# A fused convolution and feed-forward kernel: all tap products ahead of the fifth copies, part buffers in thirds, one more group on seven products

## The chip, the core and the metric

The kernel runs on one core of one Trainium2 chip. The metric is the device time of one execution in microseconds (us). Three runs of the kernel before took 988.49, 989.33 and 987.34 us, a median of 988.49. The profiled execution spans 988.2 us, and all views below are of that execution. The engines are called as the profile calls them: PE is the matrix engine (PEld its weight loads), DVE the vector engine, ACT the scalar engine, POOL the engine that here mostly issues transfers, and SP the engine that issues the plain loads and stores.

## The reference, cut to what matters

The input is x with 8 sequences of 4224 rows of 192 channels. The reference is two steps:

```
w   = softmax(weight, axis=-1)                      # 8 heads, 7 taps
y   = sum over k of w[h, k] * x_pad[s + k, channels of h]   # causal convolution, 24 channels a head
xn  = (y - mean(y)) / sqrt(var(y) + 1e-6) * g_ln
out = y + relu(xn @ w_ch1) @ w_ch2                   # 192 -> 768 -> 192
```

All numbers are float32. The two matrix products make up the arithmetic of the matrix engine. The kernel folds g_ln and the subtraction of the mean into the first weight matrix, and it multiplies by the inverse root of the variance only at the end, because relu commutes with a positive factor.

## The kernel before

**Groups.** The rows are cut into 18 groups, numbered 0 to 17; most of them hold 128 partitions times 16 rows. Groups 0 to 2 are small or odd. Groups from 3 on are "fast": their second matrix product ("down") is computed by seven products of half-size blocks instead of eight (the scheme of Strassen and Winograd). Groups 5 to 16 (`MIXED`, line 81) also compute four of the six hidden chunks of the first matrix product ("up") by seven products; the other two chunks are computed plainly. Group 4 computes its whole "up" plainly.

**What a group does.** In group g the matrix engine works first on "up" (`up`, line 538, or `up_mixed`, line 591) and then on "down" (`down_fast`, line 714). Beside that work the other engines prepare later groups and finish the earlier one:

- The convolution of group g+2 begins in "down" of group g. ACT multiplies the first tap into `y` (`first_tap`, line 376) and the second tap into a buffer `tb` (`second_tap`, line 393). When the last head of the second tap is done, POOL issues two transfers that add `tb` to `y` in halves. Line 756 to 760 say how many of these 16 ACT instructions stand behind each of the six products that are listed there.
- DVE adds the other five taps of group g+1 (`conv`, line 408) in "up" of group g, then transposes `y` into `yt`.
- ACT copies the results of the products from PSUM to SBUF, scales the output rows of group g-1 (`scale`, line 826), and POOL issues transfers that add these rows to the output in memory (`add_to_out`).
- SP stores `y` to the output and loads the next `x` (`store_y`, `load_x`).

**"Up" in mixed groups.** `up_mixed` computes its seven products in a fixed order in two sets of PSUM banks, `chain` and `other`. Three results have to be added to blocks that lie in SBUF already. For each of them ACT copies the product to a part buffer, and POOL issues a transfer that adds the buffer to the block (`close`, line 614): to c11 from a room in the pool of `tb`, to c22 from a room in the pool of `cs`, to c21 from the first room again. A room holds J * D = 3072 elements a partition, and a part uses PAIR = 2 thirds of it. After the plain chunk, DVE turns c21 and the plain chunk into relu(.) minus a block (`lower_sum`, line 702); "down" reads that in its second product.

**"Down" in fast groups.** The six calls of `product` behind line 756 are, in order: c11, c22, a part, one that stays in PSUM, c21 (the fifth) and two more. ACT copies each product's three pieces. Behind the fifth, in a mixed group, POOL issues a transfer that adds a part to c21 (`close_by_dma`, line 748, the rows `cs<-part` of the profile). `finish_fast` (line 796) then transposes the result into `ot`: its half 0 needs the rows that this transfer adds to, its half 1 needs a DVE addition first. At the end of the group DVE computes the sums of `yt` that the next mixed "up" needs (`sums_of_y`, line 575, a generator of which the last step runs inside the next "up").

**Order.** The schedule is written by hand: every engine runs its instructions in the order of the program text, and waits where a tile is not ready. POOL's queue, SP's queue and DVE's program are therefore in the order in which the Python code calls them. The pools `tb`, `cs`, `ot` and `ys` have one buffer each, `y` and `x` two.

Of the kernel before, what the change touches and what calls it, by code (L numbers as in the profile page):

```python
# [16 lines left out]
def kernel(  # L17
# [32 lines left out]
    H, K = weight.shape  # L50
# [12 lines left out]
    NQ = P // C  # L63
# [9 lines left out]
    NG = len(groups)  # L73
# [4 lines left out]
    NFAST = max(fast.values())  # L78
    T = C // 2

    MIXED = range(5, NG - 1)
    PAIR = NF // 2 - 1
    HJ = J // 2
    EARLY = 10
# [26 lines left out]
    bpool = ctx.enter_context(tc.tile_pool(name="tb", bufs=1))  # L111
    cpool = ctx.enter_context(tc.tile_pool(name="cs", bufs=1))
# [64 lines left out]
    room = hpool.tile([P, NF * J * P], F32, tag="ht", name="room")  # L177
# [213 lines left out]
    tb = {}  # L391
# [16 lines left out]
    def conv(g, k0=1, k1=K, heads=(0, H)):  # L408
        n = groups[g][2]
        t = xg[g]  # L410
        for k in range(k0, k1):
            for h in range(*heads):
                cs = slice(h * GRP, h * GRP + GRP)
                nc.vector.scalar_tensor_tensor(  # L414
                    out=y[g][:, 0:n, cs], in0=t[:, k : k + n, cs], scalar=taps[:, h, k : k + 1],
                    in1=y[g][:, 0:n, cs], op0=ALU.mult, op1=ALU.add,
                )
# [173 lines left out]
    def up_mixed(g, last_sum):  # L591


        W = HJ * C
        assert groups[g][2] == fast[g] == 2 * HJ and PAIR * W == 512
        hidden_tile(g)
        a = ht[g][0]
        a11, a12, a21, a22 = quarters_of_y(g)
        b11, b12, b21, b22 = quarters_of_w1()
        s1, s2, s3 = ysums[g]  # L600
        (c11, c12), (c21, c22) = [
            [a[:, h, e, 0:PAIR].rearrange("p f q j t -> p f q (j t)") for e in range(2)]
            for h in range(2)
        ]

        def parts(pool, tag):
            room = pool.tile([P, J * D], F32, tag=tag, name=f"parts_{tag}{g}")
            return room[:, 0 : PAIR * NQ * W].rearrange("p (f q w) -> p f q w", q=NQ, w=W)

        def evict(banks, dst, relu=False):  # L610
            src = banks.rearrange("p q (f w) -> p f q w", w=W)
            nc.scalar.activation(dst, src, AF.Relu) if relu else nc.scalar.copy(dst, src)  # L612

        def close(c, part):
            whole = "p f q w -> p (f q w)"
            add_by_dma(c.rearrange(whole), part.rearrange(whole))

        def plain(f, banks):
            rows_of_tiles(banks, yt[g][:, 0 : 2 * HJ], w1[:, :, f * P : f * P + P])
            evict_up(g, f, slice(0, 2 * HJ), banks)  # L620


        chain, other = take_set(), take_set()
        turn[0] += 4
        done = groups[g - 1][2]
        first, second = parts(bpool, "tb"), parts(cpool, "cs")
        rows_of_tiles(chain, a11, b11, True, False)
        evict(chain, c11)
        rows_of_tiles(other, a12, b21)
        evict(other, first)  # L630
        close(c11, first)
        rows_of_tiles(chain, s2, w1sums[:, 1], False, False)
        evict(chain, c21)
        scale(g - 1, 0, 1)
        conv(g + 1, 2, 3)
        next(last_sum)
        rows_of_tiles(other, s3, w1sums[:, 2], True, False)
        evict(other, c22)
        scale(g - 1, 1, 2)
        rows_of_tiles(chain, s1, w1sums[:, 0], False, False)  # L640
        evict(chain, second)
        close(c22, second)
        scale(g - 1, 2, 3)
        rows_of_tiles(other, a22, w1sums[:, 3], False)
        evict(other, first)
        close(c21, first)
        scale(g - 1, 3, 4)
        rows_of_tiles(chain, s2, b22, False)
        evict(chain, c12, True)
        nc.scalar.activation(c11, c11, AF.Relu)  # L650
        scale(g - 1, 4, 7)
        conv(g + 1, 3, 6)
        plain(PAIR, other)
        nc.scalar.activation(c22, c22, AF.Relu)
        scale(g - 1, 7, 10)
        add_to_out(g - 1, 0, 8)
        lower_sum(g, (PAIR,))
        lower_sum(g, range(PAIR))
        conv(g + 1, 6, K)
        plain(PAIR + FC, chain)  # L660
        scale(g - 1, 10, done)
        add_to_out(g - 1, 8, done)
# [51 lines left out]
    def down_fast(g):  # L714
        n = fast[g]
        t = width(g)
        w = n * T
        a = ht[g][0]
        flat = cpool.tile([P, NC, NFAST * C], F32, tag="cs", name=f"cs{g}")[:, :, 0 : n * C]
        order = "p c (h j t) -> p c h j t" if t == C else "p c (j h t) -> p c h j t"  # L720
        cs = flat.rearrange(order, h=2, t=t)
        part = cpool.tile([P, CH, NFAST * T], F32, tag="part", name=f"part{g}")[:, :, 0:w]
        part = part.rearrange("p c (j t) -> p c j t", t=t)

        parts = [part, a[:, 1, 0].rearrange("p f q j t -> p (f q) j t")[:, 0:CH]]
        banks = [take_bank() for c in range(CH) for i in range(2)]

        def product(bank, left, right, to, first):
            for c in range(CH):
                dst = banks[2 * c + bank]  # L730
                for f in range(FC):
                    for q in range(NQ):
                        nc.tensor.matmul(  # L733
                            dst[C * q : C * q + C, 0:w], right[:, f, C * c : C * c + C],
                            left[:, f, q], start=(first and f == 0), stop=(f == FC - 1),
                            skip_group_check=True,
                        )
                if to is not None:
                    nc.scalar.copy(  # L739
                        to[:, c], dst[:, 0:w].rearrange("p (j t) -> p j t", t=t)  # L740
                    )

        b = quarters_of_w2()
        c11, c21 = cs[:, 0:CH, 0], cs[:, 0:CH, 1]
        c12, c22 = cs[:, CH:NC, 0], cs[:, CH:NC, 1]
        todo = [(tap, h) for tap in (first_tap, second_tap) for h in range(H)] if g + 2 < NG else []

        def close_by_dma(c, part):
            add_by_dma(*(v.rearrange("p c j t -> p c (j t)") for v in (c, part)))

        def some_taps(times):
            for tap, h in todo[:times]:
                tap(g + 2, heads=(h, h + 1))
            del todo[:times]

        taps_behind = [3, 3, 3, 3, 2, 2]
        if g in MIXED:
            taps_behind = [1, 4, 4, 5, 2, 0]
        elif g + 1 in MIXED:
            taps_behind = [4, 4, 4, 4, 0, 0]  # L760
        product(0, a[:, 0, 0], b[0], c11, True)
        some_taps(taps_behind[0])
        product(1, a[:, 1, 0], w2sums[:, 2], c22, True)
        some_taps(taps_behind[1])
        product(1, a[:, 1, 1], w2sums[:, 3], parts[0], False)
        some_taps(taps_behind[2])
        product(1, a[:, 0, 1], b[2], None, True)
        some_taps(taps_behind[3])
        if g in MIXED:
            transpose(g + 1)  # L770
            moments(g + 1, 0, EARLY)
        elif g + 1 in MIXED:
            moments(g + 1)
            if g + 1 == MIXED[0]:
                sums_of_quarters(w1sums, *quarters_of_w1())
        half_sum(g, (1, 1), (1, 1), (1, 0), ALU.add)
        half_sum(g, (0, 0), (1, 1), (0, 0), ALU.add)
        half_sum(g, (0, 1), (0, 1), (1, 1), ALU.subtract)
        for c in range(CH):
            nc.vector.tensor_tensor(  # L780
                c11[:, c], c11[:, c], banks[2 * c + 1][:, 0:w].rearrange("p (j t) -> p j t", t=t),
                op=ALU.add,
            )
        product(0, a[:, 1, 1], w2sums[:, 1], c21, False)
        if g + 1 == NG:
            finish_fast(g, 0, flat, cs, parts)
        if g in MIXED:
            close_by_dma(c21, parts[0])
        some_taps(taps_behind[4])
        product(0, a[:, 0, 0], w2sums[:, 0], parts[1], False)  # L790
        some_taps(taps_behind[5])
        product(0, a[:, 0, 1], b[3], c12, False)
        some_taps(len(todo))
        return flat, cs, parts
# [96 lines left out]
    for g in range(NG):  # L891
        if g + 2 < NG and g not in (3, 4):
            load_x(g + 2)
        mixed, last = g in MIXED, g + 1 == NG
# [41 lines left out]
        parts = down_fast(g)  # L936
# [6 lines left out]
        if mixed:  # L943
            moments(g + 1, EARLY)
        later = sums_of_y(g + 1) if g + 1 in MIXED else iter(())
        if not last:
            finish_fast(g, 0, *parts)
            next(later, None)
        finish_fast(g, 1, *parts)
        if not last and not mixed and g + 1 not in MIXED:  # L950
            moments(g + 1)
        if not last and g % 2 == 0:
# [35 lines left out]
```

## Time and profile before

| | us or share |
|---|---|
| runs (three) | 988.49, 989.33, 987.34 |
| profiled span | 988.2 |
| PE busy | 969.5 (98%) |
| DVE busy | 854.3 (86%) |
| ACT busy | 623.3 (63%) |
| POOL busy | 178.0 (18%) |
| granted clock of the matrix engine | 0.999 |
| one "up", plain (group 4), from its first matrix instruction to that of "down" | 31.1 |
| one "up", seven products (group 5) | 28.6 |
| one mixed group (groups 5 to 16), from "up" to "up" | 56.03 to 57.47 |

The last three rows come from the timeline of PE. In the profile, "out<-in" names the tiles that an instruction writes and reads; `room` is the large tile that holds the hidden blocks, `parts_tb` and `parts_cs` are the part buffers, `ps` is PSUM. A matrix product in float32 appears as two records for each instruction of the program, so that 48 records are 24 instructions. A row of the waits reads "who waited <- who ended the wait: us in total, times, longest".

### The profile page before, as it was taken

The page shows a single profiled execution, that of the slowest core. Times are in us where ns is not written, and L with a number is a line of the kernel's source. Part 1 is how long each engine was busy: PE and PEld are TensorE (multiplying, and loading weights), DVE is VectorE, ACT ScalarE, POOL GpSimd, SP SyncE. Part 2 cuts the span into 40 slices and gives each one's busy share as a digit, 9 for nine tenths or more (in the row PEclk, how much of TensorE's full clock was granted, in tenths as well). Part 3 has the DMA queues.
Part 4 walks back from the last instruction along what each step waited for, and adds up shares of the span by engine and source line. Part 5 has one row for each costly group of instructions (what it writes and reads, how often), then busy time and mean ns, then how long its engine had stood idle before and what let it go on. Part 6 is the DMA issues. An engine that isn't in the chain of part 4 may idle for free.

```text
span 988.2 us, 35674 instructions
## 1 busy us (share of the span) xinstructions
PE 969.5 (98%) x16050; PEld 659.8 (67%) x16050; DVE 854.3 (86%) x1477; ACT 623.3 (63%) x1034; POOL 178.0 (18%) x317
## 2 busy tenths in 40 slices
PE   7999999999999999999999999999999999999997
PEld 6886445556758585766758576676857566685787
DVE  6999886899899898989999898989989898998507
ACT  5625646364867758585875858586685848675451
POOL 2002500115111041112211041111301141110200
PEclk9999999999999999999999999999999999999999
DMA  8233752664797869779677977969696786675141
GB/s 201 95 121 130 116 164 36 209 157 130 139 250 145 239 130 191 194 153 253 143 219 145 208 178 143 260 131 241 143 236 148 147 237 135 160 147 93 18 67 67
DMA packets 26279, 156.07 MB, mean 158 GB/s; under 512 B 3215, under 2 KB 8591, under 8 KB 17294
## 3 DMA queue, kind: packets, MB, share of 16 engines
q0 software_dynamic: 19456, 96.25, 50.3%
q1 hardware_dynamic: 6366, 57.54, 15.2%
q8 instruction: 126, 2.06, 0.8%
q14 instruction: 27, 0.22, 0.1%
q10 hardware_dynamic: 304, 0.00, 0.0%
HBM read 38.95 MB, written 50.33 MB: 90 GB/s over the span
## 4 chain that ended last, share of the span: by engine, by line
issue 44%; PE 32%; DMA 11%; POOL 8%; DVE 4%; ACT 2%; POOLq 0%; SPq 0%; ACTq 0%; DVEq 0%
PE ps L532 16%; PE ps L733 11%; DMA y<-tb 7%; PE ps L680 5%; DVE y L414 3%; DMA xg<-in_x_dram 2%; POOL room L589 2%; POOL out_dram L835 2%; POOL cs L589 1%; ACT parts_tb L612 1%; POOL y L403 1%; DMA room<-parts_tb 1%; POOL d L458 1%; DMA ga<-in_moe_g_ln_dram 0%; DVE room L698 0%
## 5 line engine op out<-in xcount | busy, mean ns | idle before, releaser
L414 DVE SCALAR_TENSOR_TENSOR y<-xg,taps,y 128x384 f32<-128x384 f32 (+4 forms) x734 | 368.1, 579 | 12.1 <-issue 8.9
L532 PE MATMUL ps<-yt,w 32*128 32x512 f32 (+5 forms) x4320 | 334.2, 461 | 2.9 <-ACT parts_tb L612 1.9
L532 PEld LDWEIGHTS ps<-yt,w 32*128 32x128 f32 x4320 | 213.7, 185 | 116.5 <-issue 95.4
L733 PE MATMUL ps<-room,w2sums 128*32 128x256 f32 (+2 forms) x4320 | 233.7, 374 | 0.4 <-issue 0.3
L733 PEld LDWEIGHTS ps<-room,w2sums 128*32 128x32 f32 x4320 | 140.9, 110 | 87.7 <-DVE room L698 2.3
L698 DVE TENSOR_TENSOR room<-room 128x1024 f32<-128x1024 f32 (+2 forms) x144 | 160.4, 1186 | 42.0 <-ACT part L739 23.3
L733 PE MATMUL ps<-room,w 128*32 128x256 f32 (+2 forms) x3240 | 179.3, 374 | 0.0
L733 PEld LDWEIGHTS ps<-room,w 128*32 128x32 f32 x3240 | 104.6, 110 | 72.8 <-ACT ot L828 9.1
L739 ACT COPY cs<-ps 128x256 f32<-128x256 f32 (+2 forms) x180 | 63.3, 366 | 111.8 <-PE ps L733 111.1
L522 ACT ACTIVATE room<-ps 128x2048 f32<-128x2048 f32 (+4 forms) x54 | 79.8, 1477 | 55.2 <-PE ps L532 55.1
L532 PE MATMUL ps<-ysums,w1sums 32*128 32x256 f32 x1728 | 98.4, 377 | 4.0 <-ACT parts_tb L612 4.0
L828 ACT ACTIVATE ot<-ot,r 128x192 f32<-128x192 f32 x248 | 96.2, 448 | 0.0
L532 PEld LDWEIGHTS ps<-ysums,w1sums 32*128 32x128 f32 x1728 | 87.5, 185 | 12.8 <-ACT parts_tb L612 8.3
L612 ACT COPY room<-ps 128x2048 f32<-128x2048 f32 x36 | 67.3, 1868 | 39.6 <-PE ps L532 37.1
L707 DVE SCALAR_TENSOR_TENSOR room<-room 128x1024 f32<-128x1024 f32 x36 | 43.0, 1223 | 45.0 <-ACT room L522 24.5
L387 ACT ACTIVATE y<-xg,taps 128x384 f32<-128x384 f32 (+4 forms) x137 | 71.7, 590 | 11.2 <-DMA out_dram<-y 8.5
L835 POOL DMA_DIRECT2D out_dram<-ot x40 | 34.0, 1077 | 238.2 <-ACT ot L828 187.6
L441 DVE BATCH_NORM_STATS2 st<-y 128x6 f32<-128x192 f32 x264 | 70.8, 342 | 0.0
L612 ACT COPY parts_tb<-ps 128x2048 f32<-128x2048 f32 x24 | 44.8, 1866 | 27.3 <-DMA y<-tb 18.5
L803 DVE STREAM_TRANSPOSE ot<-cs 128x512 f32<-128x512 f32 (+2 forms) x90 | 55.8, 670 | 6.2 <-DMA cs<-part 3.7
L425 DVE STREAM_TRANSPOSE yt<-y 128x3072 f32<-128x3072 f32 (+4 forms) x19 | 56.2, 2957 | 5.1 <-PE ps L532 3.0
L400 ACT ACTIVATE tb<-xg,taps 128x384 f32<-128x384 f32 x112 | 59.5, 605 | 0.0
(104 smaller groups left out, 702.4 us busy)
## 6 DMA issues: line engine op xcount, KB each, us to landing
xg<-in_x_dram SPq DMA_DIRECT2D x12, 2112.0 KB, 14.8
room<-parts_tb POOLq DMA_DIRECT2D x24, 1024.0 KB, 9.3
y<-tb POOLq DMA_DIRECT2D x28, 768.0 KB, 9.1
out_dram<-ot POOLq DMA_DIRECT2D x27, 768.0 KB, 7.8
out_dram<-y SPq DMA_DIRECT2D x12, 1536.0 KB, 9.7
room<-parts_cs POOLq DMA_DIRECT2D x12, 1024.0 KB, 7.5
cs<-part POOLq DMA_DIRECT2D x12, 384.0 KB, 4.5
xg<-in_x_dram POOLq DMA_DIRECT2D x2, 2112.0 KB, 17.8
```

The costliest lines, as they stand in the source:

```text
L387: nc.scalar.mul(dst, src, tap)
L400: nc.scalar.mul(tb[g][:, 0:n, cs], xg[g][:, 1 : 1 + n, cs], taps[:, h, 1:2])
L414: nc.vector.scalar_tensor_tensor(out=y[g][:, 0:n, cs], in0=t[:, k : k + n, cs], scalar=taps[:, h, k : k + 1], in1=y[g][:, 0:n, cs], op0=AL ...
L425: nc.vector.transpose(yt[g][:, 0:n, c0:c1].rearrange("p j c t -> p j (c t)"), y[g][:, 0:n, C * c0 : C * c1])
L441: nc.vector.bn_stats(out=sums[g][:, j, :], in_=y[g][:, j, :])
L522: nc.scalar.activation(dst, src, AF.Relu)
L532: nc.tensor.matmul(banks[:, q, i * w : i * w + w], right[rows, c, P * i : P * i + P], left[rows, :, c, :], start=(first and c == 0 and i = ...
L612: nc.scalar.activation(dst, src, AF.Relu) if relu else nc.scalar.copy(dst, src)
L698: nc.vector.tensor_tensor(a[:, *dst, f], a[:, *left, f], a[:, *right, f], op=op)
L733: nc.tensor.matmul(dst[C * q : C * q + C, 0:w], right[:, f, C * c : C * c + C], left[:, f, q], start=(first and f == 0), stop=(f == FC - 1 ...
L739: nc.scalar.copy(to[:, c], dst[:, 0:w].rearrange("p (j t) -> p j t", t=t))
L828: nc.scalar.mul(ots[g][:, j, :], ots[g][:, j, :], rstd[g][:, j : j + 1])
```

## The change

The change has five edits.

1. `MIXED` begins at group 4, so that group 4 computes "up" with seven products. The sums of the first weight matrix (`w1sums`) are then built in "down" of group 3, and the lists of taps move with it.
2. In mixed groups the fourth product is followed by seven ACT tap products instead of five, and none is left behind the fifth. So all 16 stand ahead of the copies of the fifth product, and the two transfers `y<-tb` stand on POOL's queue ahead of `cs<-part` instead of behind it.
3. The part of c21 is copied in two pieces: each goes into the unused last third of one of the two rooms, and each has a transfer of its own.
4. Half of the last tap (four of the eight heads) is computed by DVE ahead of `lower_sum` instead of behind it.
5. The three sums of `yt` are computed by DVE ahead of half 0 of `finish_fast` instead of behind it.

```
-    MIXED = range(5, NG - 1)
+    MIXED = range(4, NG - 1)
...
-            return room[:, 0 : PAIR * NQ * W].rearrange("p (f q w) -> p f q w", q=NQ, w=W)
+            return room.rearrange("p (f q w) -> p f q w", q=NQ, w=W)
...
-        first, second = parts(bpool, "tb"), parts(cpool, "cs")
+        rooms = parts(bpool, "tb"), parts(cpool, "cs")
+        first, second = (r[:, 0:PAIR] for r in rooms)
...
-        evict(other, first)
-        close(c21, first)
+        for i, room in enumerate(rooms):
+            one, third = slice(i, i + 1), room[:, PAIR : PAIR + 1]
+            evict(other, third, i=one)
+            close(c21[:, one], third)
...
         conv(g + 1, 3, 6)
+        conv(g + 1, 6, K, heads=(0, H // 2))
         plain(PAIR, other)
...
         lower_sum(g, (PAIR,))
         lower_sum(g, range(PAIR))
-        conv(g + 1, 6, K)
+        conv(g + 1, 6, K, heads=(H // 2, H))
...
         if g in MIXED:
-            taps_behind = [1, 4, 4, 5, 2, 0]
+            taps_behind = [1, 4, 4, 7, 0, 0]
...
-        if not last:
-            finish_fast(g, 0, *parts)
-            next(later, None)
-        finish_fast(g, 1, *parts)
+        next(later, None)
+        for half in range(last, 2):
+            finish_fast(g, half, *parts)
```

## The prediction

> **What bounds the kernel.** I read the shares first, then the waits, then the timeline of PE, then that of all engines across one mixed group.
>
> ```profile
> PE 969.5 (98%) x16050; PEld 659.8 (67%) x16050; DVE 854.3 (86%) x1477; ACT 623.3 (63%) x1034; POOL 178.0 (18%) x317
> ```
>
> PE is the bound; only its work and its stalls count. The waits say where it stalls:
>
> ```profile
> PE ps L532 <- ACT parts_tb L612: 5.9, 12, 1.2
> ...
> ACT parts_tb L612 <- DMA y<-tb: 18.5, 11, 2.5
> ...
> ACT parts_tb L612 <- DMA room<-parts_tb: 4.7, 3, 1.6
> ...
> DVE room L707 <- ACT room L522: 24.5, 12, 2.7
> DVE room L707 <- DMA room<-parts_tb: 20.5, 12, 2.3
> ...
> DVE ot L803 <- DMA cs<-part: 3.7, 4, 1.7
> ```
>
> PE waits for ACT's copies into the `tb` room, and ACT waits for the transfers that still read that room: 11 times `y<-tb`, 3 times the part of c11. DVE idles ahead of `lower_sum`. PE's timeline prices a group:
>
> ```profile
> 181.59 31.18 PE L532 MATMUL ps<-yt,w 32*128 32x512 f32 x288
> 212.70 4.09 PE L733 MATMUL ps<-room,w 128*32 128x256 f32 x72
> ...
> 240.31 5.46 PE L532 MATMUL ps<-yt,w 32*128 32x256 f32 x96
> 245.59 7.95 PE L532 MATMUL ps<-ysums,w1sums 32*128 32x256 f32 x144
> 253.36 2.77 PE L532 MATMUL ps<-yt,w1sums 32*128 32x256 f32 x48
> 255.95 2.77 PE L532 MATMUL ps<-ysums,w 32*128 32x256 f32 x48
> 258.54 10.48 PE L532 MATMUL ps<-yt,w 32*128 32x512 f32 x96
> 268.95 4.09 PE L733 MATMUL ps<-room,w 128*32 128x256 f32 x72
> 272.86 7.95 PE L733 MATMUL ps<-room,w2sums 128*32 128x256 f32 x144
> ```
>
> Starts count here. Plain "up": 212.70 - 181.59 = 31.1. Seven products: 268.95 - 240.31 = 28.6. Group 5 has hardly a stall and takes 56.03 (next start 296.34); groups 5 to 16 sum to 922.00 - 240.31 = 681.7, so 12 x 55.95 = 671.4 of work and some 10.3 of stalls. They are: the two ysums sections take 7.77 unstalled, but 7.96 to 9.27 in groups 6 to 16, 7.0 in sum (`y<-tb`); 0.82, 0.83 and 0.79 ahead of the plain chunk in groups 8, 11 and 14, 2.4 in sum (part of c11); the rest is scattered tenths. Last, the end of one group:
>
> ```profile
> 265.85 1.23 DVE L707 SCALAR_TENSOR_TENSOR room<-room 128x1024 f32<-128x1024 f32 x1 [2.44 <-ACT room L522]
> 269.30 2.36 DVE L707 SCALAR_TENSOR_TENSOR room<-room 128x1024 f32<-128x1024 f32 x2 [2.23 <-DMA room<-parts_tb]
> ...
> 289.38 1.30 POOL L589 DMA_DIRECT2D cs<-part  x1 [15.19 <-ACT cs L739]
> 290.39 2.10 POOL L403 DMA_DIRECT2D y<-tb  x2
> ...
> 295.39 1.90 DVE L803 STREAM_TRANSPOSE ot<-cs 128x512 f32<-128x512 f32 x3 [0.66 <-DMA cs<-part]
> ...
> 302.78 1.87 ACT L612 COPY parts_tb<-ps 128x2048 f32<-128x2048 f32 x1 [1.63 <-DMA y<-tb]
> ```
>
> The three adds on POOL's queue land at 295.27, 299.00 and 302.68 by the trace: one behind the other, and ACT waits for the last.
>
> **What the Trainium skill says.** "DMA: Bandwidth & Descriptors", section "Queues, rings and completion order": each of 16 transfer engines consumes a queue's descriptors in order and takes turns between queues by packet. The trace agrees for POOL's queue (the landings above, 3.7 apart). The same page, "Why a DMA increments its semaphore by 16 and not by 1": all engines have to finish. By the packet records 14 of 16 finish the last `y<-tb` by 300.84, but one at 302.35. The same page, "Latency and other measured facts", says that some engines are usually slower; here one lags in most transfers, and the 16 KB packets of the instruction queue may be why.
>
> **The change part by part.**
>
> *Seven products in group 4.* 31.1 - 28.6 = 2.5 saved on PE. The four sums `w1sums` (0.95 each, 3.7 at their spacing) move into group 3's DVE, between its moments and its half sums. There DVE idled 6.9 ahead of the half sums and has moments (4.2) to pull in as well, so 7.9 fills 6.9 and the half sums start about 1 late, at 167.3. PE's fifth product starts at 170.5 and needs three of them (3.2), one at a time: nothing lost, at most 0.5. On POOL the store of `y` and the load of `x` leave some 7 earlier with `y<-tb`; the memset behind the load then waits until about 192, ahead of group 4's first part transfer (189), whose block ACT needs at about 202 and which takes 7.5: 0 to 0.5. I count 2.2.
>
> *Taps.* Two ACT instructions (0.52 each at their spacing) move ahead of the fifth product's copies: the last tap ends at 286.9 instead of 290.1, the first of these copies is 0.9 late, the third, at 288.7, not. PE's sixth product begins at 288.4 with the bank copied first, so nothing is lost. `y<-tb` is issued at 287.1, 3.3 earlier and ahead of `cs<-part`, so it lands 2.5 to 4.5 earlier; ACT waited at most 2.5. The 7.0 go (6 to 7).
>
> *Thirds.* One copy of 2048 (1.87) becomes two of 1024 (about 1.0 each, from the row of a 1024 copy at L522): 0.1 on an ACT that waits 0.3 for PE there: free. POOL issues one transfer more (0.85 of an engine 18% busy). The wait on c11's part goes: 2.4.
>
> *Half a tap ahead of `lower_sum`.* 4 x 0.53 = 2.1 of DVE fills the idle 2.4 and 2.2 there. By itself it costs nothing, and it frees 2.1 later.
>
> *Sums ahead of half 0.* 2.8 of DVE work fills the wait for `cs<-part`.
>
> *What is given back.* `cs<-part` now lands last of the three. It is issued at 289.4 as before, behind 1.5 MB. Let T be its landing after the start of PE's next "up". From it DVE's path runs: 3 transposes, addition, 3 transposes (4.8), 8 taps 4.2, sum 0.9, 24 taps 12.7, and now 4 taps more, 2.1: 24.7, then three `lower_sum` of 1.15 to T + 28.2. PE needs the last of these at 272.86 - 240.31 + 0.43 = 33.0, so PE stalls by T - 4.7. Lower bound of T: the three transfers take 13.3 from first issue to last landing (289.38 to 302.68), so 287.1 + 13.3 = 300.4, T = 4.1: no stall. Upper bound: the slow transfer engine is busy without a gap from the output add to the last `y<-tb`, in group 5 with x's load until 291.3; then the order changes nothing, the last landing stays at 302.7, T = 6.3, and the stall is 1.6. By group, the gap between that load's landing and the first packets of the three adds (issue + 2.2) is 0 in group 5, 1.4, 0.3, 0.5, 1.6, 1.6, 1.1, 0.8, 1.5, 1.2 in 6 to 14; there is no load in 15. Taking it from the last landings (5.9 to 7.2 after the next "up" starts) and summing what is above 4.7 gives 7.3 for all groups. But a stall also moves PE's next start, and so takes itself from the next T: half, 3.6, where the slow engine has no gap. I take 4.2.
>
> **Sum.** 988.2 - 7.0 - 2.4 - 0.5 (scattered) - 2.2 + 4.2 = 980.3 against the profile's span; the span stands 0.3 below the median of the runs, so I forecast 980.
>
> **Rivals.**
> (a) *Nothing is given back*: T stays near 4.1. For it: the data are the same and start 3.3 earlier. Against: the packets of the slow engine. 988.2 - 9.9 - 2.3 = 976.
> (b) *Most is given back*: the slow engine has no gap in any group, stall 0.8 a group in 11 groups: 976 + 9 = 985.
> (c) *Slower*: the add of c21 ends the wait. If T stays at 6.3 whatever PE does, the stall is 1.6 in 11 groups, 17.6, against 12.2 saved: 993.5. It decides from T = 4.7 + 12.2 / 11 = 5.8. For it: the last landing now is 5.9 to 7.2 after the "up". Against: the gaps, and that landings are paced by the previous "up", not by the stalled "down".
> (d) *The thirds or early taps don't move the wait*, and group 4 alone gains: 986. Against: POOL's order of issue shows `y<-tb` first.
>
> **How the numbers follow.** Likeliest, partly given back (977.5 to 983.5): 0.45; (a) 0.25; (b) 0.14; (c) 0.11, with a part of it near no change; (d) 0.05. The range 975.5 to 987 leaves out most of (c) and the tail of (a). A measurement of this kernel tells 0.2% (2 us) from no change: faster 0.84, same 0.07, slower 0.09.
>
> **What would show it.** Right: the waits of ACT for `y<-tb` and for `room<-parts_tb` are gone; group 4's "up" takes 28.6 to 29.2; DVE waits for `cs<-part` at L808 in all mixed groups, 3 to 6 each, and hardly ahead of `lower_sum` (L712); some groups show PE waiting for DVE at its second "down" product, up to 1. Wrong: PE waits there in all groups for over 1, or ACT's scaling of the output waits for DVE in the next "up", or the first ysums section still takes over 8.

## The result and the profile after

The changed kernel took 977.22 us (median of four runs, 976.89 to 978.04), the kernel before 988.91 in the same comparison, 11.7 us more. The ratio is 0.9885, with a 95% interval from 0.9867 to 0.9902: 1.15% faster. The profiled span is 975.6 us.

The page's first line after, engine by engine:

```profile
PE 961.7 (99%) x16194; PEld 665.4 (68%) x16194; DVE 854.3 (88%) x1480; ACT 633.9 (65%) x1052; POOL 188.5 (19%) x334
```

DVE's work is the same to a tenth (854.3 us). The span is 12.6 us shorter: PE's busy time fell by 7.8 and its idle time by 4.8. The busy figure doesn't part work from stalls here, because a row of matrix instructions that is held up for some tenths still counts as busy (before, the rows lost 9.4 us to `parts_tb`, 7.0 and 2.4, of which the list of waits has 5.9). The starts of PE's rows do, and they follow below. All waits of PE over the whole execution (who waited <- who ended it: us in total, times, longest):

```profile
PE ps L364 <- POOL room L292: 4.9, 1, 4.9
PE ps L329 <- DVE room L245: 1.7, 1, 1.7
PE ps L738 <- issue: 1.0, 1, 1.0
PE ps L532 <- DVE yt L425: 0.7, 1, 0.7
PE ps L320 <- DMA xg<-in_x_dram: 0.5, 1, 0.5
```

The wait for ACT's copies into `parts_tb` has left the list, and nothing has come in its place: L364, L329 and L320 are the set-up ahead of group 0, the wait of 0.7 for `yt` stood in the list before with the same figure, and the wait of 1.0 is in the last group. The chain that ended last says it in another way. Here is its first line after:

```profile
PE 95%; DVE 2%; DMA 2%; issue 0%; ACT 0%; SPq 0%
```

Before, that line began with "issue 44%; PE 32%; DMA 11%; POOL 8%": the chain ran back through transfers and through time in which an engine waited for nothing that the profile shows ("issue"). Now it runs almost wholly through PE. PE's timeline in groups 4 and 5:

```profile
180.95 5.46 PE L532 MATMUL ps<-yt,w 32*128 32x256 f32 x96
186.24 7.95 PE L532 MATMUL ps<-ysums,w1sums 32*128 32x256 f32 x144
...
209.59 4.09 PE L738 MATMUL ps<-room,w 128*32 128x256 f32 x72
213.50 7.95 PE L738 MATMUL ps<-room,w2sums 128*32 128x256 f32 x144
...
236.93 5.46 PE L532 MATMUL ps<-yt,w 32*128 32x256 f32 x96
242.21 7.95 PE L532 MATMUL ps<-ysums,w1sums 32*128 32x256 f32 x144
249.98 2.77 PE L532 MATMUL ps<-yt,w1sums 32*128 32x256 f32 x48
252.57 2.77 PE L532 MATMUL ps<-ysums,w 32*128 32x256 f32 x48
255.16 10.48 PE L532 MATMUL ps<-yt,w 32*128 32x512 f32 x96
265.57 4.09 PE L738 MATMUL ps<-room,w 128*32 128x256 f32 x72
```

Group 4's "up" now takes 209.59 - 180.95 = 28.6, as group 5's does (265.57 - 236.93). Every group from 4 to 16 takes 55.97 or 55.98 from start to start; before, groups 5 to 16 took 56.03 to 57.47. So the account is: groups 5 to 16, 681.7 to 671.7, 10.0 less; group 4, 58.7 to 56.0, 2.75 less; 0.65 less ahead of group 4 and 0.8 more behind group 16. The sum is 12.6 less, as the spans say. The 0.65 lies ahead of the first "up" and the 0.8 in the last group; these runs explain neither.

The end of group 5, from the timeline of all engines after:

```profile
283.74 1.74 POOL L403 DMA_DIRECT2D y<-tb  x2 [12.93 <-ACT cs L744]
...
285.93 1.28 POOL L589 DMA_DIRECT2D cs<-part  x1 [0.46 <-ACT cs L744]
...
296.80 1.90 DVE L808 STREAM_TRANSPOSE ot<-cs 128x512 f32<-128x512 f32 x3 [4.28 <-DMA cs<-part]
...
298.47 1.87 ACT L613 COPY parts_tb<-ps 128x2048 f32<-128x2048 f32 x1 [0.77 <-PE ps L532]
```

`y<-tb` leaves 2.2 us ahead of `cs<-part`. ACT's copy at L613 waits for PE now, no longer for a transfer. DVE waits 4.28 for `cs<-part`, where it waited 0.66. DVE's idle time has moved rather than gone: ahead of `lower_sum` it was 45.0 us in all (24.5 and 20.5 in the waits before) and is 3.2 now, while the waits for `cs<-part` have grown from 3.7 to this:

```profile
DVE ot L808 <- DMA cs<-part: 40.6, 10, 4.4
```

These waits cost PE nothing: DVE's chain from the wait to `lower_sum` still ends in time, as its own timeline shows for group 5's "up", behind the end of group 4:

```profile
240.80 1.90 DVE L808 STREAM_TRANSPOSE ot<-cs 128x512 f32<-128x512 f32 x3 [4.06 <-DMA cs<-part]
...
245.46 4.28 DVE L414 SCALAR_TENSOR_TENSOR y<-xg,taps,y 128x384 f32<-128x384 f32 x8
...
250.53 14.91 DVE L414 SCALAR_TENSOR_TENSOR y<-xg,taps,y 128x384 f32<-128x384 f32 x28
265.35 3.49 DVE L712 SCALAR_TENSOR_TENSOR room<-room 128x1024 f32<-128x1024 f32 x3
268.76 2.20 DVE L414 SCALAR_TENSOR_TENSOR y<-xg,taps,y 128x384 f32<-128x384 f32 x4
```

`lower_sum` (L712) has no idle time ahead of it in this group. Its last instruction ends at 268.8. PE wants the last block 0.43 after the start of the second product of "down" (the time of the eight records that need only the block before it), and that product begins 213.50 - 209.59 = 3.91 after the start of "down": at 265.57 + 3.91 + 0.43 = 269.9. That leaves some 1.1 us.

### The profile page after: what moved, and what is told of

Same layout as the page of the kernel before. It is cut to its first block, busy times and chain, and to the rows that moved or that the text cites. A ratio compares the mean times of both kernels' runs of the same rounds, so it can differ in the third digit from the quotient of the medians.

```text
span 975.6 us, 36012 instructions
## 1 busy us (share of the span) xinstructions
PE 961.7 (99%) x16194; PEld 665.4 (68%) x16194; DVE 854.3 (88%) x1480; ACT 633.9 (65%) x1052; POOL 188.5 (19%) x334
## 4 chain that ended last, share of the span: by engine, by line
PE 95%; DVE 2%; DMA 2%; issue 0%; ACT 0%; SPq 0%
PE ps L532 48%; PE ps L738 41%; PE ps L685 5%; DMA xg<-in_x_dram 2%; DVE y L414 2%; PE ps L320 1%; DMA ga<-in_moe_g_ln_dram 0%; DVE yt L425 0%; PE ps L345 0%; DVE y L847 0%; PE ps L350 0%; PE ps L332 0%; DVE y L389 0%; ACT w L355 0%; DVE ot L872 0%
## 5 line engine op out<-in xcount | busy, mean ns | idle before, releaser
L532 PE MATMUL ps<-yt,w 32*128 32x256 f32 (+5 forms) x4224 | 318.7, 453 | 0.7 <-DVE yt L425 0.7
L532 PEld LDWEIGHTS ps<-yt,w 32*128 32x128 f32 x4224 | 209.0, 185 | 102.7 <-issue 84.7
L703 DVE TENSOR_TENSOR room<-room 128x1024 f32<-128x1024 f32 (+2 forms) x141 | 156.9, 1184 | 35.4 <-ACT part L744 24.9
L532 PE MATMUL ps<-ysums,w1sums 32*128 32x256 f32 x1872 | 103.3, 374 | 0.0
L613 ACT COPY room<-ps 128x2048 f32<-128x2048 f32 x39 | 72.8, 1867 | 45.3 <-PE ps L532 43.9
L532 PEld LDWEIGHTS ps<-ysums,w1sums 32*128 32x128 f32 x1872 | 95.9, 185 | 5.1
L522 ACT ACTIVATE room<-ps 128x2048 f32<-128x2048 f32 (+4 forms) x50 | 72.2, 1444 | 39.4 <-PE ps L532 39.3
L685 PE MATMUL ps<-room,w 128*32 128x192 f32 (+3 forms) x1152 | 59.4, 366 | 0.0
L403 POOL DMA_DIRECT2D y<-tb x28 | 24.6, 1037 | 175.0 <-ACT cs L744 154.8
```

The source lines that it names most:

```text
L532: nc.tensor.matmul(banks[:, q, i * w : i * w + w], right[rows, c, P * i : P * i + P], left[rows, :, c, :], start=(first and c == 0 and i = ...
L685: nc.tensor.matmul(bank[C * q : C * q + C, 0:w], w2[:, f, C * c : C * c + C], t[:, f, q, js.start - fast[g] : js.stop - fast[g], :], start ...
L703: nc.vector.tensor_tensor(a[:, *dst, f], a[:, *left, f], a[:, *right, f], op=op)
```

## The experiments

The experiments ran on three other chips, on which the kernel before took 992.5 to 992.7 us, and in the profiled executions there the first "up" begins 2 to 5 us later than in the two profiles above. So two numbers are given: the ratio to the kernel before on the same chip, and the time from the start of group 4 to the start of group 17 in the profiled execution ("thirteen groups"), which leaves the start out. Thirteen groups take 740.4 us before and 727.7 after; both are from the profiles above.

**The changed kernel again** (no edit).

> The changed kernel once more, unaltered, so that its time stands beside the other runs on the same chip. Every group from 4 to 16 should take 55.97 to 55.98 us again, and the ratio to the kernel before lie at 0.9885 within its interval.

Measured: 980.03 us, ratio 0.9879 (0.9860 to 0.9899), thirteen groups 728.1. Twelve groups took 55.97 to 55.98, and one took 56.41. So a stray stall of 0.4 can happen, and by these two executions 0.4 is what a difference of thirteen groups has at least to exceed.

**Group 4 plain.**

```
-    MIXED = range(4, NG - 1)
+    MIXED = range(5, NG - 1)
```

> The changed kernel with group 4's first product computed plainly again (MIXED from 5). Theory (each edit's saving adds up on PE): group 4 costs 31.1 instead of 28.6 us for "up", so the time is 2.5 to 2.8 us over the changed kernel, about 980. Rival (the saving in group 4 is swallowed by the sums that DVE computes earlier, in group 3): no difference, 977.

Measured: 982.53 us, ratio 0.9908 (0.9892 to 0.9924), thirteen groups 730.6. Group 4 takes 58.74 instead of 55.97, 2.8 more; the others are as in the changed kernel within 0.1. The theory holds, and the sums that moved into group 3 cost nothing (group 3 takes 54.84 in both).

**Last taps late again.**

```
-            taps_behind = [1, 4, 4, 7, 0, 0]
+            taps_behind = [1, 4, 4, 5, 2, 0]
```

> The changed kernel with the last two taps behind the copies of the fifth product again ([1, 4, 4, 5, 2, 0]), everything else as changed. Theory (y<-tb landed too late, and its place in the issue order cures it): the transfers land 6 us after the start of the next "up" again, PE stalls 0.2 to 1.5 a group, 6 to 7 in sum, about 984. Rival (DVE's freed 2 us make the transfers ahead of them earlier, and y<-tb would land in time anyhow): 977 to 979.

Measured: 987.61 us, ratio 0.9953 (0.9939 to 0.9968), thirteen groups 734.8, 7.1 over the changed kernel. The waits of ACT and PE in this run:

```profile
ACT parts_tb L613 <- DMA y<-tb: 19.6, 12, 2.3
...
PE ps L532 <- ACT parts_tb L613: 3.8, 9, 1.0
```

The loss is where it was before the change: PE's rows `ps<-ysums,w1sums` lose 7.1 in sum in groups 5 to 16. The second `y<-tb` lands 5.8 to 7.0 us after the start of the next "up", as before the change, although the store and the load in front of it start 2 to 4 us earlier in the group than in the kernel before. So the late taps are the cause, and the rival falls. The edit moves two things at once, the time at which `y<-tb` can be issued and its place behind `cs<-part`; no run parts them. As an estimate from the landings in group 5: the last of the three adds lands 6.34 after the next start in the kernel before and 3.77 in the changed one, which is 2.6 for the earlier start of all three, and in the changed kernel the second `y<-tb` lands at 1.79, another 2.0 for its place.

**One part for c21.**

```
-        for i, room in enumerate(rooms):
-            one, third = slice(i, i + 1), room[:, PAIR : PAIR + 1]
-            evict(other, third, i=one)
-            close(c21[:, one], third)
+        evict(other, first)
+        close(c21, first)
```

> The changed kernel with c21's part copied whole into the first room again, one transfer instead of two. Theory of the prediction (the thirds remove a wait worth 2.4 us): about 979.6, with PE stalls of about 0.8 ahead of the plain chunk in three groups. Rival (that wait was a consequence of the late y<-tb, because c11's transfer was itself issued late): with y<-tb early, c11's transfer lands 15.3 to 16.4 us after the start of "up" and the copy starts at 15.9, so next to nothing remains, 977 to 978.

Measured: 986.35 us, ratio 0.9944 (0.9930 to 0.9957), thirteen groups 733.9, 6.2 over the changed kernel. Both expectations are too low. Groups 5 to 16 account for 2.6, in steps of up to 1.0 where c11's transfer lands late, near the prediction's 2.4. The other 3.6 are in group 4. Its timeline in this run:

```profile
189.55 1.87 ACT L613 COPY parts_tb<-ps 128x2048 f32<-128x2048 f32 x1 [0.77 <-PE ps L532]
...
194.57 1.05 POOL L160 MEMSET xg<- 1x1152 f32 x1 [17.46 <-DMA xg<-in_x_dram]
...
195.57 0.59 POOL L589 DMA_DIRECT2D room<-parts_tb  x1
...
203.81 1.87 ACT L613 COPY parts_tb<-ps 128x2048 f32<-128x2048 f32 x1 [4.26 <-DMA room<-parts_tb]
...
205.73 6.72 PE L532 MATMUL ps<-yt,w 32*128 32x512 f32 x60 [3.34 <-ACT parts_tb L613]
```

The part is ready at 191.4, but POOL stands at the memset behind the load of x until 194.6 and issues the transfer only then. ACT needs the room back, waits 4.26, and PE waits 3.34. In the changed kernel the memset is as late, but nobody needs the room: thus the thirds carry the mixed group 4 as well. (Group 5's share of the 2.6, 0.7, may be an after-effect of this.)

**The last tap behind `lower_sum`.**

```
-        conv(g + 1, 6, K, heads=(0, H // 2))
...
-        conv(g + 1, 6, K, heads=(H // 2, H))
+        conv(g + 1, 6, K)
```

> The changed kernel with the whole last tap behind lower_sum again. Theory (the half tap matters because the store and load behind it start earlier, which clears the transfer engines for cs<-part): the load of x lands about 1.2 us later and cs<-part lands up to 5 us after the start of "up" instead of 3.9; lower_sum itself has 2.1 us more room, so PE stalls hardly, 977 to 979. Rival (DVE has no room left: the idle time ahead of lower_sum is lost, half sums come late for PE's fifth product): PE waits up to 0.7 a group, up to 985.

Measured: 981.90 us, ratio 0.9895 (0.9877 to 0.9912), thirteen groups 727.7, as in the changed kernel; every group takes 55.97 or 55.98. (The 1.9 us between the medians here and in the repeat of the changed kernel are in the start: in the profiled executions the first "up" begins 1.9 later, behind a granted clock of 0.50 from 14.8 to 21.6 that the repeat does not have.) So half a tap ahead of `lower_sum` buys nothing here. Nor did the part of the theory on transfers hold: in group 6 the load of x lands 1.0 later than in the changed kernel, and `cs<-part` lands at 4.1 after the next start instead of 4.0; the largest landing in any group is 4.14, not 5. What the half tap does do is take room. Group 5 starts at 241.65 in this run, and DVE runs its `lower_sum` as follows:

```profile
267.95 2.36 DVE L711 SCALAR_TENSOR_TENSOR room<-room 128x1024 f32<-128x1024 f32 x2
270.74 1.23 DVE L711 SCALAR_TENSOR_TENSOR room<-room 128x1024 f32<-128x1024 f32 x1 [0.43 <-DMA room<-parts_cs]
```

So it ends 30.3 after the start of the group, with the half tap 31.9, and PE wants it at 33.0.

**Half 0 ahead of the sums.**

```
-        next(later, None)
-        for half in range(last, 2):
-            finish_fast(g, half, *parts)
+        if not last:
+            finish_fast(g, 0, *parts)
+            next(later, None)
+        finish_fast(g, 1, *parts)
```

> The changed kernel with half 0 of finish_fast ahead of the sums of yt again, so that the sums wait for cs<-part. Theory (early taps are possible only because the sums were moved out of that wait): cs<-part lands 3.9 us after the start of "up", three transposes and two sums later, at about 7.7, s2 is ready, while PE wants it at 5.3; a stall of about 2.4 in 12 groups, 29 us, about 1006. Rival (there is room, moving the sums is decoration): 977 to 980.

Measured: 1020.09 us, ratio 1.0283 (1.0252 to 1.0314), thirteen groups 768.7, 41 over the changed kernel, 2.5 to 4.7 in each of groups 5 to 16. PE's list of waits has a new row:

```profile
PE ps L532 <- DVE ysums L582: 29.2, 12, 2.9
```

In the timeline, at the end of group 5:

```profile
302.26 1.90 DVE L808 STREAM_TRANSPOSE ot<-cs 128x512 f32<-128x512 f32 x3 [6.86 <-DMA cs<-part]
...
305.03 0.96 DVE L582 TENSOR_TENSOR ysums<-ysums,yt 128x768 f32<-128x768 f32 x1
...
306.13 9.74 PE L532 MATMUL ps<-ysums,w1sums 32*128 32x256 f32 x144 [2.31 <-DVE ysums L582]
```

The sum of L582 is ready 7.6 after the start of "up" (298.36), as expected, and PE waits 2.2 to 2.9. Some 12 us came on top, which neither theory had. PE's last row above takes 9.5 us to its successor at 315.66 instead of 7.8, and the windows view of PE (length of the stretch, busy us and instructions, granted clock, share and rate of the transfers) says why:

```profile
299.00:304.00 5.00, 4.82 (x92) 1.00 0.36 58
304.00:306.00 2.00, 0.00 (x0) 1.00 0.00 0
306.00:308.00 2.00, 1.87 (x29) 0.86 0.32 66
308.00:310.00 2.00, 2.00 (x24) 0.50 0.96 197
310.00:312.00 2.00, 2.00 (x33) 0.79 1.15 238
312.00:314.00 2.00, 2.00 (x44) 1.00 0.18 37
```

The number behind the brackets is the granted clock: after the stall it falls to half for some microseconds. It does so in five of the twelve groups, at some 1.8 us each, 9 in all; the other 3 us are 0.2 to 0.3 a group by which the loss exceeds the listed wait. The groups with the fall are easily told: those that take 60.2 to 60.7 us have a mean granted clock of 0.97 (this one about the same, from the rows above), the others 1.00 and 58.5 to 59.2; the next group, with a stall of 2.91, is one of the latter. Without the moved sums, early taps are a large loss.

**A small and a large dose ahead of `cs<-part`.** Both add stores of rows that are stored already, four or eight of 16 a partition:

```
         if g in MIXED:
+            for ps, rows in rows_of_out(g + 1, 0, 4):      # 8 in the large dose
+                nc.gpsimd.dma_start(
+                    out=rows, in_=y[g + 1][ps, 0:4].rearrange("p j d -> p (j d)")
+                )
             close_by_dma(c21, parts[0])
```

> The changed kernel with one more transfer on POOL's queue ahead of cs<-part in every mixed group: it stores 4 of the 16 rows a partition of the next y once more (384 KB). It moves T, the landing of cs<-part after the start of PE's next "up", and adds no work on PE, DVE or ACT. The prediction's step says that PE stalls by T - 4.7. If the transfer moves T from 3.9 by 1 to 2, to 4.9 to 5.9, PE stalls 0.2 to 1.2 in 12 groups: 979 to 991. Rival (the path from cs<-part to lower_sum has more room than that): 977 to 978.

> As the small dose, with 8 rows (768 KB). T should move by 2 to 3.7, to 5.9 to 7.6, and by the prediction's step PE stalls 1.2 to 2.9 in 12 groups: 991 to 1012, by then no longer faster than the kernel before. Rival (more room than 0.8): the stall is smaller than T - 4.7 by that room.

Measured: small dose 982.77 us, ratio 0.9903 (0.9878 to 0.9928), thirteen groups 729.2; large dose 994.03 us, ratio 1.0020 (1.0010 to 1.0030), thirteen groups 741.1. T, the landing of `cs<-part` after the start of the next "up", and the length of that next group over 55.97:

| | T | next group's excess |
|---|---|---|
| changed kernel, groups 4 to 15 | 3.75 to 4.00 | 0.00 to 0.01 |
| small dose, group 10 | 4.93 | 0.15 |
| small dose, group 6 | 4.95 | 0.17 |
| small dose, group 5 | 5.02 | 0.27 |
| small dose, group 4 | 5.27 | 0.53 |
| large dose, group 5 | 5.68 | 0.93 |
| large dose, group 4 | 5.82 | 1.08 |
| large dose, group 12 | 6.15 | 1.40 |

In the rows with a dose the excess is T - 4.75 within 0.03, and in all 24 groups of the two runs (nothing where T is under 4.75) it is so within 0.05. T moved less than expected: by 0.7 to 1.5 with the small dose, by 1.8 to 2.4 with the large one. In PE's timeline of the small dose the stall sits where the prediction put it, in the second product of "down" of group 5:

```profile
272.69 0.61 PE L738 MATMUL ps<-room,w2sums 128*32 128x256 f32 x8
273.63 7.55 PE L738 MATMUL ps<-room,w2sums 128*32 128x256 f32 x136 [0.32 <-DVE room L712]
```

PE runs one block of eight records and waits for the next block of `lower_sum`. With the large dose a second wait joins it:

```profile
ACT room L613 <- DVE cs L810: 16.5, 12, 1.7
...
PE ps L738 <- DVE room L712: 6.0, 12, 0.5
```

ACT's copy into c21's block waits until DVE has added the part of the last "down" (`finish_fast`, half 1), because that part lies in the same block, and PE loses 0.1 to 0.7 in its row `ps<-ysums,w1sums` behind it. The loss at the second product of "down" is then 0.71 in every group, so the sum is still T - 4.75. With the large dose, at a T of 5.66 to 6.20 (mean 5.9), the thirteen groups take 0.7 more than in the kernel before: the gain of the whole change is gone, as rival (c) was worked out to have it from a T of 5.8.

**Early taps and sums alone**, in the kernel before:

```
-            taps_behind = [1, 4, 4, 5, 2, 0]
+            taps_behind = [1, 4, 4, 7, 0, 0]
...
-        if not last:
-            finish_fast(g, 0, *parts)
-            next(later, None)
-        finish_fast(g, 1, *parts)
+        next(later, None)
+        for half in range(last, 2):
+            finish_fast(g, half, *parts)
```

> The kernel before with two edits alone: the early taps and the sums ahead of half 0. Theory (these two are what matters in groups 5 to 16; whole parts cost 2 to 2.6 there, and half a tap nothing): groups 6 to 16 take 56.0 to 57.0 with a sum of about 2 over the changed kernel's, and with group 4 plain (2.8) the time is 4.5 to 5 us over the changed kernel. Group 4's cost of whole parts (3.6 us) doesn't appear, since its part transfers are gone. Rival (the half tap is needed once the part of c21 comes in one piece): PE waits for DVE at its second product in "down", more than 1 a group.

Measured: 983.10 us, ratio 0.9914 (0.9896 to 0.9932), thirteen groups 731.5. Group 4 is plain (58.6), groups 5 to 16 are 1.2 over the changed kernel's. These two edits bring 8.9 of the 12.7 us of the thirteen groups. The time is 3.1 over the repeat of the changed kernel, and the thirteen groups are 3.9 over, less than the 4.5 to 5 that were expected. PE does not wait for DVE at the second product of "down": the rival falls. What is left of its waits for `parts_tb` is one, for the part of c11 in group 11, which takes 56.77:

```profile
PE ps L532 <- ACT parts_tb L612: 0.5, 1, 0.5
```

**Thirds alone**, in the kernel before (edit 3 as in the change).

> The kernel before with the part buffers in thirds alone. Theory (the thirds take away the wait for c11's part, 2.4 us in three groups, and leave the wait for y<-tb): groups 8, 11 and 14 lose their 0.8 ahead of the plain chunk, the time falls by 2 to 3 us. Rival (the wait for y<-tb and that for the part trade places: what is removed from one comes back in the other): no difference.

Measured: 989.11 us, ratio 0.9974 (0.9956 to 0.9992), thirteen groups 737.5, 2.9 under the kernel before. ACT's waits in this run show `y<-tb` alone:

```profile
ACT parts_tb L612 <- DMA y<-tb: 18.1, 11, 2.1
```

The wait for `room<-parts_tb` (4.7 before) is gone, the other has stayed (18.5 before). PE's rows say the same: ahead of the plain chunk `ps<-ysums,w` takes 2.59 in every group, also in 8, 11 and 14, where it took 3.4, and the rows `ps<-ysums,w1sums` lose 6.7 in sum, 7.0 before. The two waits are separate, and the thirds take away one of them.

## Why the prediction was right, and which term was mis-sized

The forecast was 980 and the time 977.2: inside the range, faster as forecast, with a gain of 11.7 us where 8.5 was forecast. What was called likeliest, that part of the gain is given back, did not come; rival (a) did, to which a chance of 0.25 was given. By its steps:

*Seven products in group 4: right, a little low.* 2.2 was counted; 2.7 to 2.8 came (2.5 in "up" and 0.3 of stall in "down"). The late memset was seen, but sized at 0 to 0.5; the run with one part shows that it is worth 3.6 where the thirds don't absorb it.

*Taps: right.* 7.0 was counted, and undoing them costs 7.1. (The row that the prediction calls two sections holds three products.)

*Thirds: right in groups 5 to 16.* 2.4 was counted; undoing them costs 2.6 there, doing them alone gains 2.9 in the thirteen groups.

*Half a tap and the moved sums.* Costing the first at nothing was right; what it "frees later" turned out to be worth nothing too, and it takes 1.6 of the room ahead of `lower_sum`. The sums were costed as filling a wait. The run without this edit shows that they are more than that: they are the condition for the early taps.

*What is given back: the mis-sized term.* 4.2 was counted, 0 came. The threshold was right: PE stalls by T - 4.7 was worked out (its own figures, 33.0 - 28.2, give 4.8), T - 4.75 was measured. The wrong number was the upper bound of T, 6.3, and with it the middle value. It rested on the statement that the slow transfer engine is busy without a gap up to the last add, so that the order of the three adds changes nothing. T came out at 3.75 to 4.00 in groups 4 to 15, 0.1 to 0.35 below the lower bound of 4.1. Three observations go against the statement: group 15 has no load of x and has T = 3.75, hardly less than the groups with one; in the run with the last tap behind, a load that lands 1.0 later moves T by 0.2; and with early taps and sums alone the store of group 5's "down" is issued as late as before, 35.6 after the start of the group, and T is still 3.8. Engines do lag: by the completion records of the changed kernel in group 5, 14 of 16 engines end the load by 285.9 and the last at 287.1, and 13 of 16 end the last add by 295.3 and the last at 296.7. But that is one lag of 1.3 to 1.4 in both places, not one on top of the other; why it does not add up is not shown. What held is the sum of the lower bound: in groups 4 to 15 the first add is issued 46.8 after the start of the group, and the last lands 12.9 to 13.2 later. The trace of before held the answer: its three adds took 12.9 to 13.3 from first issue to last landing in ten of eleven groups (14.2 in group 14), among them 13.2 in group 15, which has no load either.

*A stall takes itself from the next T: not so with the large dose.* There PE stalls 0.9 to 1.4 in each group and T stays at 5.7 to 6.2 throughout: `cs<-part` is issued behind the fifth product, which is stalled with everything else (issue at about 50.1 instead of 49.0 after the start of the group). With the small dose T does fall, from 5.27 in group 4 to 4.73 in group 9, with the time from issue to landing (12.2 to 11.7); why is open.

*Rivals.* What came is (a), at 976 against a measured span of 975.6. (b) did not come: the sign that the prediction named, PE waiting for DVE at the second product of "down", shows in no group of the changed kernel. (d) falls with the runs that undo the taps and that do the thirds alone. (c) named the point from which the change would lose, and the large dose puts it where it was worked out.

## What to carry to other kernels

Where a bound engine waits for a transfer, look first at what stands ahead of that transfer in the queue that issues it; issuing `y<-tb` 3.3 us earlier and ahead of the other transfer moved its landing by 4.5 us in group 5 here, and it paid only because the work that would have waited behind the other one was reordered in the same change. Price the wait that such a swap creates by the chain from it to the next instruction that the bound engine needs: it had 0.8 to 1.0 us of room here (T of 3.75 to 4.00 against 4.75), and within that room a wait of 4.3 us costs nothing. And before assuming that transfers crowd each other, look for a stage in the same trace in which the suspected one is missing.

## What the runs showed that was not expected

PE's clock can fall after a stall: in the run with half 0 ahead of the sums, an idle time of 2.3 us was followed by a granted clock of 0.50 and cost another 1.8. The Trainium skill ("TensorE: Matmul & The Clock Gate", "What's actually happening") describes a clock that halves after an idle window of about 3.4 us and says that the window runs freely; here a shorter idle time was enough, and a slightly longer one, 2.9, in the next group was not followed by it. The clock record of the trace says which stalls were. While PE works through the groups, the clock falls at 307.43, 426.90, 546.37, 723.86 and 901.35, each time to 0.50 for 3.41 us, and the distances between these falls are 35, 35, 52 and 52 times 3.413: they lie on one grid. In the stretch of 3.41 us that ends at each of the five falls PE was idle for 2.1 to 2.4. The seven other stalls, of 2.2 to 2.9, lie across a line of the grid, and no stretch has more than 1.8 of idle time. The stall of 3.3 in the run with one part lies across a line as well (1.7 and 1.6, with the grid counted from that run's own clock record) and was not followed by a fall. So in these runs the place of a stall on the grid decided, and not its length alone; where between 1.8 and 2.1 the limit lies is not shown. The rows that were held up by up to 1.5 in the kernel before show no fall (granted clock 1.00 from 9.8 to 986.0).

A buffer that is needed again soon makes the queue of the engine that drains it a hazard: one memset of 1.05 us that waits for a load held up a transfer by 4.2 us (191.4 to 195.6) and PE by 3.3 in the run with one part. And the landing of `cs<-part` is steadier than the load on the transfer engines suggests: 10.7 to 11.0 us after its issue in groups 5 to 14, with a load of x ahead of it, and 10.7 in group 15 without one. Since PE now runs groups 4 to 16 without a stall that its rows show, no reordering in them is left to gain from unless it also takes work off PE; what remains is ahead of group 4 and behind group 16, and none of these runs touched it.
